# A retention and SwiGLU kernel on one core: the first head pair in chunks of 128 tokens, with its loads, weight roundings and first products reordered

## The chip, the cores and the metric

The kernel runs on one core of a Trainium2 chip. The core has a matmul engine (PE, whose weight loads are shown apart as PEld), a vector engine (DVE), an activation engine (ACT), a general engine (POOL) and a sequencer that mostly issues transfers (SP). Each engine works through its own list of instructions in order; semaphores order the engines among each other. PE writes only to PSUM, of which this kernel uses six tiles: four banks of 512 columns (bankA, bankB, bankC, bankE) and two of 1024 columns (inner and outer). Transfers are issued by SP, ACT and POOL and are carried by 16 DMA engines.

The metric is the time of one execution on the device, in microseconds (us). Every time below is in us unless it is marked otherwise.

## The reference, cut to what matters

The kernel computes a causal retention with a decay per head, puts the heads side by side, and feeds the result to a gated feed-forward block.

```python
# q, k, v: (8, 8, 576, 64) float32      batch, heads, tokens, head size
scores = scale * np.matmul(q, k.transpose(0, 1, 3, 2))
gamma = 1.0 - 2.0 ** (-5.0 - np.arange(H))
Dmat = np.where(rel >= 0, gamma[:, None, None] ** rel, 0.0)      # rel = row - column
attn_out = np.matmul(scores * Dmat, v)
x = attn_out.transpose(0, 2, 1, 3).reshape(B * S, H * D)         # (4608, 512)
g = x @ w_gate                                                   # (512, 1536)
out = (g / (1.0 + np.exp(-g)) * (x @ w_val)) @ w_out             # (1536, 512)
```

The three weight matrices arrive as 64-bit floats. The kernel makes 32-bit values out of them on the chip.

## The kernel before

**Tiles of tokens.** The 4608 tokens are worked in five tiles: a first one of 512 tokens, then four of 1024. The first tile uses plain matmuls and goes on while the weights still come in. The later ones use a scheme with fewer products and prepared sums of weights.

**Retention.** Heads are taken in pairs; the four pairs of a batch (HP = 4) fill the 128 partitions twice over. Pairs 0 to 3 belong to the first batch, and their first 512 tokens are the first tile. A pair is worked in chunks of 64 tokens (L = 64): scores inside a chunk, a state carried from chunk to chunk, and the share of all earlier chunks through that state. The functions are `transposes` (q and k are turned on PE with the identity, copied out of PSUM, and the keys are scaled by the decay), `scores`, `new_states`, `masked` (the decay mask on DVE and the chain of states), `own_values`, `earlier_values` and `to_x` (the copy into `xs[0]`, which holds the input of the feed-forward block, 128 features for each pair).

**Order at the start.** `tick(t, 0, HP)` for t from 0 to 5 is a pipeline over the four pairs: in tick t, pair t is turned, pair t-1 gets its scores and states, and pair t-2 its values. For pair 0 the copies, the scaling of keys and a copy of states are on DVE. For pairs 1 to 3 (`scaled`) the rows of q are scaled ahead of their transposes by POOL (`scale_run`, L735).

**Weights.** `load_w(m)` (L370) brings a quarter-megabyte or megabyte piece of the 64-bit weights into one of three raw places; the order of pieces is the list `order`, and I write w0, w1, and so on for its entries. `split(j)` takes half a piece apart with two activations (L389, L390) on ACT, and `rounding(j)` puts the halves together on DVE (L406, L407) and, unless it is told not to, goes on with `split(j+1)`. After the second half of a piece, `split` issues the load of the piece that takes its place. So w4 is issued by SP, behind the loads of pair 4, and w5, w6 and later ones by ACT.

**The first up stage.** `up0(f, chunks)` makes the products of output block f (12 of them, gate and value each) with the feature chunks named. A product of 128 features with 512 tokens is two PE rows in the trace. Blocks 0 and 2 and so on use bankA and bankB; blocks 1, 3 and so on bankC and bankE. With the last chunk it also issues the Silu (L856) and the product with the value half (L857), which free the two banks. Blocks 0 and 1 are started with chunks 0 and 1 amid the ticks, and finished with chunks 2 and 3 after them. Block 2 follows, then block 3, then the fifth pair's `new_states` and `scores`, then block 4. Blocks 2 and on need later pieces of the weights, and the fifth pair is loaded by `load(4)`, the sixth by `load(5)` (L282 and L287, both on SP).

**Order of issue.** The engines' lists are written out by hand: what stands earlier in the program stands earlier on its engine. Transfers issued by SP and ACT share eight completion semaphores. The trace shows that a transfer waits at issue until the previous one on the same semaphore has landed.

The lines below are at the center of both the change and the reading that follows.

Of the kernel before, what the change touches and what calls it, by code (L numbers as in the profile page):

```python
# [17 lines left out]
ALU = mybir.AluOpType  # L18
# [4 lines left out]
def tables(gamma, scale, L):  # L23

    g, at = np.array(gamma), np.arange(L)
    lane = np.arange(2 * L)[:, None]
    both = lambda t: np.repeat(t, L, axis=0).reshape(-1, 2 * L, t.shape[1]).transpose(1, 0, 2).reshape(2 * L, -1)
    twice = lambda t: np.concatenate([t, t])
    half = [np.repeat(g.reshape(-1, 2), L, axis=1).T ** (lane % 32 + 32 * r) for r in range(2)]
    pieces = scale * np.stack(half, axis=2).reshape(2 * L, -1)
    runs = scale * (g[None, :, None] ** ((4 * lane[:, :, None] + np.arange(4)) % L)).reshape(2 * L, -1)
    parts = [twice((g[:, None] ** -at).T), twice((g[:, None] ** (L - at)).T),
             both(g[:, None] ** L), both(g[:, None] ** (2 * L)), pieces, runs, both(scale * g[:, None] ** at),
             both((scale * g[:, None] ** at).reshape(-1, 2, L)[:, ::-1].reshape(-1, L))]  # L40
    return np.concatenate(parts, axis=1).astype(np.float32)
# [90 lines left out]
def kernel(  # L132
# [39 lines left out]
    L = D  # L172
# [74 lines left out]
    def scaled(i):  # L247

        return 0 < i < HP
# [4 lines left out]
    def load(i):  # L254
# [6 lines left out]
        if i < HP:  # L261
# [9 lines left out]
            for h, queue in zip(heads, queues):  # L271
                queue.dma_start(out=blocks(kn)[:, h % 2], in_=k[b, h, 0:CW].rearrange("(c p) d -> p c d", p=P))
            for h in heads:
                queues[i % 2].dma_start(out=blocks(t)[:, h % 2], in_=v[b, h, 0:CW].rearrange("(c p) d -> p c d", p=P))
        else:
# [33 lines left out]
    decays = nc.inline_tensor(table, name="decays").ap()  # L309
    NCOL = 6 * H + 4 * HP  # L310
    nc.sync.dma_start(out=tab[:, 0:NCOL], in_=decays[:, 0:NCOL])
    load(0)
    load(1)
    ident = const.tile([P, P], F32, name="ident")
    make_identity(nc, ident)
    nc.scalar.activation(out=io[:, 0:1], in_=ident[:, 0:1], func=AF.Silu)
    inv, key = tab[:, 0:H], tab[:, H : 2 * H]
    step = tab[:, 2 * H : 2 * H + 2 * HP]
    piece = tab[:, 2 * H + 2 * HP : 2 * H + 4 * HP]
    run = tab[:, 2 * H + 4 * HP : NCOL]  # L320
    qry, qry_odd = [tab[:, NCOL + HP * L * n : NCOL + HP * L * (n + 1)].rearrange("p (h i) -> p h i", h=HP) for n in range(2)]
# [9 lines left out]

    even_heads, odd_heads = slice(0, H, 2), slice(1, H, 2)
    for rows in half:
        decay(slice(0, H), slice(0, H), rows)

    load(2)
    nc.sync.dma_start(out=tab[:, NCOL:], in_=decays[:, NCOL:])
    load(3)

# [70 lines left out]

    for f in range(2):
        for m in range(2):
            load_w(m, (f,))
    load_w(2)
    load_w(3)

# [26 lines left out]

    def vector(i):

        return i == 0

    def transposes(i):
# [5 lines left out]

        copy = nc.scalar.copy if i else nc.vector.tensor_copy
        if i < HP:

            mine = (bankC, bankE) if i + 1 == HP else (bankB, bankA)
            parts = [(kT, kn, mine[0]), (qT, qk, mine[1])]
            if i == 0:  # L460
                parts.reverse()

            def turn(t, src, bank):
                for c in range(NFULL):
                    to = bank[:, c : 4 * P : NFULL] if t is qT and scaled(i) else bank[:, ts(c, P)]
                    nc.tensor.transpose(to, src[:, ts(c, P)], ident)

            def put(t, _, bank):
                if i or t is qT:
                    copy(t[:, 0:CW], bank)  # L470
                else:
                    copy(t[:, 0 : CW // 2], bank[:, 0 : CW // 2])
                    nc.scalar.copy(t[:, CW // 2 : CW], bank[:, CW // 2 :])

            if i + 1 == HP:
                for part in parts:
                    turn(*part)
                pieces = [lambda part=part: put(*part) for part in parts]
            else:
                for part in parts:  # L480
                    turn(*part)
                    put(*part)
        else:
# [12 lines left out]
        def keys():  # L496
# [5 lines left out]
            for hl, rows, at in parts:  # L502
                scale = key[rows, 2 * p + hl : 2 * p + hl + 1]
                if vector(i) or 1 < i < HP:
                    (nc.vector if vector(i) else nc.gpsimd).tensor_scalar(out=at, in0=at, scalar1=scale, scalar2=None, op0=ALU.mult)
                else:
                    nc.scalar.activation(out=at, in_=at, func=AF.Copy, scale=scale)

        if light(i):
            return [lambda: (keys(), pieces[0]())] + pieces[1:]  # L510
        return [keys] + pieces

# [63 lines left out]
    def masked(i):  # L576
# [6 lines left out]
        def copies():  # L583
            (nc.vector.tensor_copy if vector(i + 1) else nc.scalar.copy)(out=even, in_=z[:, 0])

# [144 lines left out]
    def scale_run(i):  # L730
        if scaled(i):
# [3 lines left out]
            nc.gpsimd.tensor_tensor(out=dst, in0=src, in1=table, op=ALU.mult)  # L735

    def tick(t, lo=HP, hi=NP, spread=False, then=None):
        go_on(len(pieces))
        if hi == HP:

            def new_pair():
                scores(t - 1, True)
                new_states(t - 1)
                pieces.extend(masked(t - 1))
                go_on(3)

            scale_run(t + 1)
            if lo < t < hi:
                new_pair()
            if lo <= t - 2 < hi:  # L750
                own_values(t - 2)
            for f in transposes(t) if lo <= t < hi and t + 1 < HP else ():
                f()
            if lo <= t - 2 < hi:
                earlier_values(t - 2)
                if t == HP:
                    up0(0, range(2))
                to_x(t - 2)[0]()
            if t + 1 == HP:
                split(0)  # L760
                after = transposes(t)
                rounding(0)
                for f in after:
                    f()
            if t == HP:
                rounding(2)
                rounding(3, False)
                new_pair()
                while held:
                    held.pop()()  # L770
                split(4)
                up0(1, range(2))
            return
        if lo <= t - 2 < hi:
# [66 lines left out]

    def up0(f, chunks):

        pair = banks[2 * (f % 2) : 2 * (f % 2) + 2]
        for gv, bank in enumerate(pair):
            for c in chunks:
# [577 lines left out]

    for t in range(HP + 2):
        tick(t, 0, HP)

        if t == 3:
            load(HP)
        for j in {3: (1,), 5: (4, 5)}.get(t, ()):  # L1430
            rounding(j)
    for c in range(2, HP):
# [133 lines left out]
```

## Time and profile before

| What | Value |
|---|---|
| Median of three runs | 1017.77 (1017.63 to 1018.7) |
| The profiled execution | 1019.25 |
| Its span, first to last instruction | 1017.5 |
| PE busy | 1001.9 (98% of the span) |
| DVE, POOL, ACT busy | 713.2, 564.4, 285.5 |
| DMA mean rate over the span | 191 GB/s |

The span is what the profile's views divide up, and 1.75 us lie around it in the profiled execution. A busy share of 98% doesn't mean that PE is always the limit: what an earlier start is worth is decided stage by stage, by which wait ends last. The page's second part cuts the span into 40 slices of 25.4 us, and PE is below nine tenths only in the first. The views used below are the table of stretches (busy time of each engine between two times), the list of waits, the chain of work that ended last, the list of instructions in order of time, and the DMA view of a stretch.

### The profile page before, as it was taken

The numbers are of one execution on the slowest core, as the hardware profiler recorded it, in microseconds if no ns is written. First come the engines' busy times: TensorE is split into PE (matmuls) and PEld (weight loads), VectorE is DVE, ScalarE is ACT, GpSimd is POOL, SyncE is SP. The second block draws the span as 40 slices with busy tenths as digits, with TensorE's granted clock in tenths as the row PEclk, the third lists the DMA queues.
The fourth block names the chain that finished last, engine by engine and source line by source line (L and its number), as shares of the span: only waits on it lengthen the run. The fifth ranks groups of instructions, "written<-read, shape, count | busy, mean of one in ns | idle before, by whom it ended". The sixth has DMA issues, their size and how long they took to land.

```text
span 1017.5 us, 21317 instructions
## 1 busy us (share of the span) xinstructions
PE 1001.9 (98%) x8336; PEld 825.5 (81%) x8336; DVE 713.2 (70%) x1203; ACT 285.5 (28%) x636; POOL 564.4 (55%) x591
## 2 busy tenths in 40 slices
PE   6999999999999999999999999999999999999998
PEld 5644455888888888888888888888888888888887
DVE  4478889678785765967768678866575767566644
ACT  4465622132423312133322101233320012232110
POOL 3400339979575318575565248756672586566515
PEclk9999999999999999999999999999999999999999
DMA  9999887777587887657677777434454554445653
GB/s 241 253 253 241 218 241 253 203 236 218 126 252 192 232 205 215 191 167 197 184 202 204 183 186 202 165 127 165 165 176 142 149 192 146 144 155 181 185 156 100
DMA packets 278892, 194.38 MB, mean 191 GB/s; under 512 B 212552, under 2 KB 246088, under 8 KB 278792
## 3 DMA queue, kind: packets, MB, share of 16 engines
q1 hardware_dynamic: 251464, 94.70, 36.5%
q10 hardware_dynamic: 26688, 97.92, 29.1%
q8 instruction: 66, 1.08, 0.5%
q0 software_dynamic: 640, 0.39, 0.2%
q14 instruction: 34, 0.28, 0.1%
HBM read 154.04 MB, written 38.93 MB: 190 GB/s over the span
## 4 chain that ended last, share of the span: by engine, by line
PE 83%; DMA 5%; DVE 4%; SPq 3%; ACT 2%; POOL 2%; issue 1%; ACTq 1%; DVEq 0%; POOLq 0%
PE bankB L1186 11%; PE bankC L1186 11%; PE bankA L1186 11%; PE bankE L1186 11%; PE bankB L1381 7%; PE bankC L1381 7%; PE bankE L1381 6%; PE bankA L1381 6%; PE inner L1186 2%; PE outer L1186 2%; DMA qk<-in_q_dram 1%; POOL rest L1042 1%; PE outer L532 1%; PE outer L559 1%; PE inner L573 1%
## 5 line engine op out<-in xcount | busy, mean ns | idle before, releaser
L1042 POOL TENSOR_TENSOR rest<-rest 128x512 f32<-128x512 f32 (+1 forms) x141 | 150.3, 1077 | 160.8 <-DVE rest L1042 113.2
L1201 POOL TENSOR_TENSOR arena<-rest,io 128x256 f32<-128x256 f32 x168 | 123.8, 748 | 90.9 <-ACT io L1200 86.3
L1200 ACT ACTIVATE io<-rest 128x256 f32<-128x256 f32 x192 | 79.1, 417 | 202.1 <-DVE rest L1042 134.1
L1186 PE MATMUL bankB<-rest,arena 128*128 128x256 f32 x448 | 114.7, 380 | 0.1
L1042 DVE TENSOR_TENSOR rest<-bankB,rest 128x512 f32<-128x512 f32 x116 | 78.6, 686 | 42.0 <-PE bankB L1186 29.5
L1186 PE MATMUL bankC<-rest,arena 128*128 128x256 f32 x416 | 106.4, 380 | 0.1
L1186 PE MATMUL bankA<-rest,arena 128*128 128x256 f32 x412 | 104.8, 379 | 0.0
L1042 DVE TENSOR_TENSOR rest<-bankC,rest 128x512 f32<-128x512 f32 x110 | 74.6, 685 | 39.3 <-PE bankC L1186 25.3
L1042 DVE TENSOR_TENSOR rest<-bankA,rest 128x512 f32<-128x512 f32 x110 | 74.6, 686 | 37.5 <-PE bankA L1186 18.9
L1042 DVE TENSOR_TENSOR rest<-bankE,rest 128x512 f32<-128x512 f32 x106 | 71.9, 685 | 36.8 <-PE bankE L1186 17.6
L1186 PE MATMUL bankE<-rest,arena 128*128 128x256 f32 x372 | 94.9, 380 | 0.6 <-DVE rest L1042 0.6
L1186 PEld LDWEIGHTS bankB<-rest,arena 128*128 128x128 f32 x448 | 84.6, 190 | 12.5 <-DVE rest L1042 0.7
L1186 PEld LDWEIGHTS bankC<-rest,arena 128*128 128x128 f32 x416 | 78.5, 190 | 11.9 <-DVE rest L1042 1.3
L1186 PEld LDWEIGHTS bankA<-rest,arena 128*128 128x128 f32 x412 | 78.1, 190 | 10.9 <-DVE rest L1042 0.2
L1186 PEld LDWEIGHTS bankE<-rest,arena 128*128 128x128 f32 x372 | 70.3, 190 | 10.7 <-DVE rest L1042 1.2
L1042 POOL TENSOR_TENSOR arena<-arena 128x256 f32<-128x256 f32 (+1 forms) x76 | 70.0, 943 | 9.0 <-PE bankC L1186 7.6
L886 POOL TENSOR_TENSOR rest<-rest 128x512 f32<-128x512 f32 x21 | 29.1, 1408 | 77.5 <-DVE rest L407 60.5
L1381 PE MATMUL bankB<-arena 128*128 128x256 f32 x264 | 61.0, 381 | 0.0
L1381 PE MATMUL bankE<-arena 128*128 128x256 f32 x264 | 60.8, 380 | 0.0
L1381 PEld LDWEIGHTS bankE<-arena 128*128 128x128 f32 x264 | 50.0, 190 | 6.9
L1381 PEld LDWEIGHTS bankB<-arena 128*128 128x128 f32 x264 | 49.8, 190 | 6.9
L1381 PE MATMUL bankA<-arena 128*128 128x256 f32 x240 | 55.3, 380 | 0.0
(267 smaller groups left out, 1879.0 us busy)
## 6 DMA issues: line engine op xcount, KB each, us to landing
arena<-up ACTq DMA_DIRECT2D x63, 896.0 KB, 4.7
arena<-dn ACTq DMA_DIRECT2D x65, 384.0 KB, 3.1
arena<-dn SPq DMA_DIRECT2D x39, 384.0 KB, 3.3
out_dram<-rest SPq DMA_DIRECT2D x31, 256.0 KB, 3.4
qk<-in_q_dram SPq DMA_DIRECT2D x108, 72.0 KB, 3.2
qk<-in_k_dram SPq DMA_DIRECT2D x108, 72.0 KB, 3.3
dn<-rest SPq DMA_DIRECT2D x26, 256.0 KB, 3.0
up<-arena SPq DMA_DIRECT2D x13, 512.0 KB, 5.8
```

What stands on the lines that cost most here:

```text
L532: m = nc.tensor.matmul(value(i, hl, c), s["v"][rows, at], ret[rows, c % 2 if whole(i) else hl, c // 2], start=start, stop=start, skip_grou ...
L559: nc.tensor.matmul(xr[half[hl]] if c + 1 == NC else value(i, hl, c), state[half[hl], c, :], s["qT"][half[hl], ts(c, L)], start=False, stop ...
L573: nc.tensor.matmul(sc[chunk(i, hl, 2 * c + r)[0], r if whole(i) else hl, c], kT[half[hl], at], qT[half[hl], at], start=True, stop=True, sk ...
L886: eng.tensor_tensor(out=dst, in0=srcs[0], in1=srcs[1], op=ALU.add if op[0] == "add" else ALU.subtract)
L1042: eng.tensor_tensor(out=out, in0=a, in1=b, op=ALU.add if sign > 0 else ALU.subtract)
L1186: m = nc.tensor.matmul(b[:, g * TB : (g + 1) * TB], w[:, g], x, start=(opens and g == 0), stop=True, skip_group_check=True)
L1200: nc.scalar.activation(out=s, in_=src[:, 0:TB], func=AF.Silu)
L1201: (nc.vector if busy and o != 2 and qd + 1 < NQ else nc.gpsimd).tensor_tensor(out=hid[:, qd, 2 * H + h, 2 * T + t], in0=src[:, TB : 2 * TB ...
L1381: nc.tensor.matmul(b[:, m * TB : (m + 1) * TB], lhs[:, qd, ts(m, P)], w[:, qd], start=(opens and qd == 0 and m == 0), stop=(qd == NQ - 1), ...
```

## The change

It touches the first 40 us of the program and nothing after it.

**Pair 0.** Three tables are added to the decay constants: `first_inv`, `first_key` (two columns each) and `first_qry` (128 columns). Pair 0 leaves the pipeline of ticks and gets functions of its own that use four chunks of 128 tokens where the others use eight of 64. `first_scores` turns q and k into bankE and bankC, multiplies q by `first_qry` while it is copied, scales the keys on DVE, and makes 8 score products of 128 by 128 in place of 16 of 64 by 64, masked in two DVE instructions with `first_near`, which POOL makes. `first_states` makes 8 state products into bankA, with one copy and three steps of the state chain. `first_own` makes 8 products, `first_out` 6, and one ACT copy puts the result into `xs[0]`.

**Loads.** The first table transfer moves behind pair 0's first q and k. The v loads of pairs 0 and 1 come after the q and k loads of both. Pair 3's loads come after the first halves of w0 and w1, and the second table transfer after w2.

**Order.** The ticks are replaced by a list written out. In it the transposes of pairs 1, 2 and 3 all go to bankC and bankE, and their two copies come ahead of the scaling of keys. The roundings of the first two halves come around pair 2's scores. The four products of block 0 with chunks 0 and 1 are spread: one ahead of pair 1's earlier values, two behind pair 3's transposes, one behind pair 2's earlier values.

```diff
@@ load(i), pairs 0 to 3
             for h, queue in zip(heads, queues):
                 queue.dma_start(out=blocks(kn)[:, h % 2], in_=k[b, h, 0:CW].rearrange("(c p) d -> p c d", p=P))
-            for h in heads:
-                queues[i % 2].dma_start(out=blocks(t)[:, h % 2], in_=v[b, h, 0:CW].rearrange("(c p) d -> p c d", p=P))
+                if i == 0 and queue is nc.sync:
+                    nc.sync.dma_start(out=tab[:, 0:NCOL], in_=decays[:, 0:NCOL])
+
+            def values():
+                for h in heads:
+                    queues[i % 2].dma_start(out=blocks(t)[:, h % 2], in_=v[b, h, 0:CW].rearrange("(c p) d -> p c d", p=P))
+
+            loaded[i] = (qk, kn, t)
+            return values
@@ set-up
-    NCOL = 6 * H + 4 * HP
-    nc.sync.dma_start(out=tab[:, 0:NCOL], in_=decays[:, 0:NCOL])
-    load(0)
-    load(1)
+    NCOL = 6 * H + 4 * HP + 4 + P
+    values = [load(0), load(1)]
     ident = const.tile([P, P], F32, name="ident")
     make_identity(nc, ident)
     nc.scalar.activation(out=io[:, 0:1], in_=ident[:, 0:1], func=AF.Silu)
+    for f in values:
+        f()
+    load(2)()
...
-    load(2)
-    nc.sync.dma_start(out=tab[:, NCOL:], in_=decays[:, NCOL:])
-    load(3)
...
-    for f in range(2):
-        for m in range(2):
-            load_w(m, (f,))
+    for m in range(2):
+        load_w(m, (0,))
+    load(3)()
+    for m in range(2):
+        load_w(m, (1,))
     load_w(2)
+    nc.sync.dma_start(out=tab[:, NCOL:], in_=decays[:, NCOL:])
     load_w(3)
@@ new functions for pair 0
+    def first_scores():
...
+        for src, bank in ((qk, bankE), (kn, bankC)):
+            for c in range(NFULL):
+                nc.tensor.transpose(bank[:, ts(c, P)], src[:, ts(c, P)], ident)
...
+        nc.vector.tensor_tensor(out=blocks(qT), in0=blocks(bankE), in1=table(first_qry), op=ALU.mult)
+        nc.vector.tensor_copy(kT[:, 0 : CW // 2], bankC[:, 0 : CW // 2])
+        nc.scalar.copy(kT[:, CW // 2 : CW], bankC[:, CW // 2 :])
...
+        for c, hl in first:
+            nc.tensor.matmul(inner[:, hl, ts(c, P)], kT[half[hl], ts(c, P)], qT[half[hl], ts(c, P)],
+                             start=True, stop=True, skip_group_check=True)
+        for hl in range(2):
+            nc.vector.tensor_tensor(out=first_ret[:, hl], in0=blocks(inner[:, hl]), in1=table(first_near[:, ts(hl, P)]), op=ALU.mult)
@@ the order of the start
-    for t in range(HP + 2):
-        tick(t, 0, HP)
-
-        if t == 3:
-            load(HP)
-        for j in {3: (1,), 5: (4, 5)}.get(t, ()):
-            rounding(j)
+    scale_run(1)
+    first_scores()
+    scale_run(2)
+    turn_pair(1)
+    first_states()
+    first_own()
+    new_pair(1)
+    turn_pair(2)
+    first_out()
+    split(0)
+    rounding(0, False)
+    scale_run(3)
+    new_pair(2)
+    own_values(1)
+    split(1)
+    up0(0, [0], [0])
+    earlier_values(1)
+    to_x(1)[0]()
+    put = transposes(3)
+    rounding(1, False)
+    for f in put:
+        f()
+    load(HP)
+    up0(0, [1], [0])
+    up0(0, [0], [1])
+    split(2)
+    own_values(2)
+    earlier_values(2)
+    up0(0, [1], [1])
+    to_x(2)[0]()
+    rounding(2)
+    rounding(3, False)
+    new_pair(3)
+    while held:
+        held.pop()()
+    split(4)
+    up0(1, range(2))
+    own_values(3)
+    earlier_values(3)
+    to_x(3)[0]()
+    for j in (4, 5):
+        rounding(j)
     for c in range(2, HP):
         for f in range(2):
             up0(f, [c])
```

## The prediction

> **What bounds the kernel now.** I read the table of stretches first, because a PE busy share of 98% hides where its few idle microseconds lie.
>
> ```profile
> core 0: us, PE busy (x) PEld busy (x) DVE busy (x) ACT busy (x) POOL busy (x), PEclk, DMA share, GB/s
> 0.00:4.40 4.40, 0.00 (x0) 0.01 (x1) 0.00 (x0) 0.00 (x0) 2.16 (x10) 1.00 0.62 138
> 4.40:23.00 18.60, 15.40 (x376) 12.93 (x376) 11.18 (x27) 8.79 (x19) 7.16 (x7) 1.00 1.16 259
> 23.00:41.00 18.00, 17.42 (x184) 8.93 (x185) 9.00 (x18) 11.16 (x24) 7.57 (x16) 1.00 1.00 269
> 41.00:58.00 17.00, 15.88 (x127) 11.93 (x126) 6.94 (x13) 6.90 (x14) 4.99 (x9) 1.00 0.90 187
> 58.00:127.00 69.00, 68.02 (x726) 34.47 (x724) 58.37 (x121) 42.31 (x79) 9.35 (x7) 1.00 0.94 249
> 127.00:1017.50 890.50, 885.17 (x6926) 757.18 (x6926) 627.74 (x1028) 216.37 (x505) 533.16 (x545) 1.00 0.62 184
> ```
>
> The DMA engines are as good as full from 4.4 to 58 (shares 1.16, 1.00, 0.90; transfers overlap, so a share can pass 1). PE loses 4.4 + 3.2 + 0.6 + 1.1 = 9.3 us there, and little later. So the change works on 9.3 us at most, and the transfers run full just where it wants to be faster. Next, PE's waits up to 60 us:
>
> ```profile
> PE bankA L466 <- POOL near L328: 4.4, 1, 4.4
> PE bankA L853 <- ACT io L856: 1.1, 1, 1.1
> PE outer L532 <- ACT rest L389: 1.1, 1, 1.1
> PE inner L573 <- ACT rest L470: 0.9, 2, 0.7
> ```
>
> The second row decides: it is at 57.41, where block 4 of the up stage begins, and an earlier start can be lost there. ACT's and PE's instructions around it:
>
> ```profile
> 52.80 0.67 ACT L389 ACTIVATE rest<-rest 128x512 f32<-128x512 f32 x1 [6.18 <-DMA rest<-in_moe_w_gate_dram]
> 55.63 0.69 ACT L389 ACTIVATE rest<-rest 128x512 f32<-128x512 f32 x1 [0.45 <-ACT rest L390]
> 56.77 0.59 ACT L856 ACTIVATE io<-bankA 128x512 f32<-128x512 f32 x1
> 57.41 3.70 PE L853 MATMUL bankA<-rest,arena 128*128 128x512 f32 x8 [1.12 <-ACT io L856]
> ```
>
> Block 4 needs bankA, which the Silu of block 2 reads. bankA was full at 44.8, but the Silu stands on ACT behind three splits, and the first of them waits for w4. The chain of waits has the same piece: w4's load, 43.95 to 52.69, then ACT.
>
> ```profile
> 41.31 2.54 SPq L287
> 43.86 0.05 issue
> 43.92 0.03 issue
> 43.95 8.74 DMA rest<-in_moe_w_gate_dram
> ```
>
> So block 4 starts at w4's landing plus 4.7 (57.41 - 52.69), if PE is there by then. PE was there at 56.3.
>
> **The change part by part.**
>
> *Pair 0.* Its 132 matmul rows become 68: 8 transposes stay, 32 + 32 + 32 + 28 become 16 + 16 + 16 + 12. Score products have half the number and twice the columns, so they cost the same (1.13 at the early pace). States fall from 1.08 to some 0.55, own values from 1.08 to 1.0, earlier values from 0.68 to 0.5: about 0.8 us of PE, in a stretch where PE idles 3.2. DVE trades one mask of 0.69, a pairing of 0.47, three chain steps and an evens step of 0.48 for two masks of 0.69, a copy of some 0.25 and three steps of 0.28; ACT loses a copy of 0.37. No DVE row shows a 512-wide copy with a table factor out of PSUM beyond the mask's 0.69, so I take 0.69; from the plain copy (also 0.69) to the slowest vector row of that size, 1.64, it lies between 0 and +1 us, hidden if block 4 stays the meeting point.
>
> *Loads.* SP and ACT issue the same transfers in another order. Near the start 128 KB land every 0.51 us. The first table grows from 64 to 196 columns: 68 KB, 0.27 us more for all that queues behind. It lands at about 5.6 and not 2.9, ahead of the copy that needs it (5.7). POOL waits for it too: new mask, two old ones (0.68 each), then pair 1's scaling at 7.7, which started at 8.58 before. Pair 3's q lands near 17.9 in place of 14.2, behind four weight quarters of 0.85 each; the halves of w0 and w1 needed first land near 15.3 and 17 in place of 19.7 and 21.2.
>
> *The walk to block 2*, with row durations, each engine in its new order. Pair 0's scores start at 6.9 (7.47 before): q landed 3.6, two sets of transposes of 1.09 each, copy by 6.4, half of k by 6.8. Pair 1 is turned by 10.2 (11.6); pair 0's states and own values follow to 11.8, then pair 1's scores (12.3 before). Pair 2's scores run at 16.3 (17.4). ACT then splits the first half (16.9 to 18.0; two rows start 0.57 apart), DVE rounds it by 19.1 (0.42 + 0.69). The first of the four products runs at 19.1, and only then pair 1's earlier values. Pair 3 is turned from 20.7 to 22.0, which is 0.8 later than before (20.1 to 21.2), as the product stands ahead of it. Two products follow by 23.7, pair 2's values by 25.1, the fourth product by 26.0. All four products lie in time in which PE waited or worked on the same four from 23.7 to 27.4. Pair 3's scores come at 26.0 (27.36), block 1's first products at 27.3 (29.05); their value half waits for ACT's fourth split and DVE until 28.5. Pair 3's values end at 32.1 (34.17), so block 2 starts at 39.0 in place of 41.14. Gain there: 2.1 us. Hidden in it: splits on ACT wait for weights with the copies of pairs 2 and 3 queued behind them; if the halves land 1 us later than I have them, 1 of the 2.1 goes.
>
> *What is late next.* PE would reach block 4 at 54.2. With w4 landing at 52.69 it would wait 3.2 there instead of 1.1, and the gain would be zero. So the sum is w4's landing. w4 stands on SP behind the same transfers as before (pairs 0 to 4, w0 to w3), w5 and w6 go on ACT's queue ahead of its landing as before, and the engines were full: order alone moves nothing. Two things do: the table's 68 KB, +0.27, and the program itself.
>
> ```profile
> q8 instruction: 66, 1.08, 0.5%
> q8 instruction: 1, 0.02, 0.9%
> ```
>
> The page's row is 66 transfers of 16 KB; PE's 16672 rows make 253 for each, so these are PE's instructions. The second row is the DMA view from 44 to 53: one block at 44.6, 0.9% of 16 engines for 9 us = 1.3 us of one engine, while w4 waits in line. w4's sixteen parts landed from 49.09 to 52.70, against 46.01 to 47.61 for the transfer just ahead: one engine lags. Pair 0 now has 264 - 136 = 128 fewer PE rows, half a block, so the block fetched at 44.6 is asked for some 128 rows later. Those rows end in the fifth pair's products at 55, behind w4. That takes 1.3 off the lagging engine if it is the one that fetched: between 0 and -1.3, and I take -1.3 because the lag grew by 2.0 just there. Sum: +0.27 - 1.3 = -1.0 us at w4 and at block 4. From 57.41 to 126 PE has no other wait, so I carry it to the end. Both ends of what is unknown: PE can gain no more than 1.1 + 2.1 = 3.2 at block 4; and a later w4 costs in full.
>
> [...] The rows give 259 and 269 GB/s with the engines full. [...]
>
> **The rivals.**
>
> *The whole start passes on.* If w4 lands 3 us or more sooner, PE's own time decides block 4: -3.2 us, 1014.6. For it: the share falls to 0.65 of full between 28 and 30, when SP is stuck behind a lagging engine, and w5 may be issued some 2 us sooner into that gap. Against it: the lag of that one engine never goes to zero from 15 to 53. [...]
>
> *A transfer's turn gets worse: slower.* SP and ACT share eight completion semaphores, and a transfer waits for the one that had its semaphore before.
>
> ```profile
> SPq L287 <- DMA rest<-in_moe_w_out_dram: 12.4, 2, 7.9
> ```
>
> Here pair 5's v load sat 7.9 us on SP until another load had landed; it landed at 70.2, and PE used it at 71.6. The new order deals the semaphores differently. If w4, or what stands ahead of it, waits so, w4's landing moves and block 4 with it, one for one; the new slack of PE doesn't help. It decides from a hold of 1.0 us, which takes back the forecast's gain, and ends above 0.2% from 3.0. The nearest rows are issues held 3.5 and 3.9 us on SP between 34 and 44. One more of 3.5: -1.0 + 3.5 = +2.5, 1020.3. Against it: most holds end in transfers that queue anyway.
>
> *The start isn't earlier at all*, ACT being held by splits that wait for weights. Up to 3.2 us of that costs nothing at block 4, so it ends with my forecast.
>
> **How the numbers follow.** The profiled execution took 1019.25 with a span of 1017.5; it is 1.48 above the median of the runs, 1017.77. Less 1.0: span 1016.5, profiled 1018.2, median 1016.8. That case, from no gain to -2.0 (1015.8 to 1017.8), gets 0.44, the whole start 0.31, the worse turn 0.25. The range has to reach into both: from 1013.9, the whole start with 0.7 us of the later wait at 127.28 (1.25, DVE's product) gone as well, to 1020.4. 0.2%, 2.0 us, is about what a measurement can tell from no change. Faster by more: 0.32; within: 0.44; slower by more: 0.24.
>
> **What would show it.** Right: block 2 starts near 39, PE's wait before block 4 grows to 2 us or more, still on the Silu, w4 lands near 51.7, and no 16 KB block is fetched between 40 and 52. Wrong: w4 landing before 50 or after 54, block 4 waiting for something other than that Silu, block 2 no earlier than 41, or a new PE wait between block 4 and 127 us.

## The result, and the profile after

The changed kernel takes 1024.38 us (median of 6 runs, 1021.61 to 1025.77) against 1017.70 for the kernel before on the same chip (6 runs). The ratio is 1.0069, with a 95% interval of 1.0056 to 1.0082. It is slower, by 5.7 to 8.3 us. The prediction was 1016.8, with a range up to 1020.4: wrong in size and in sign. The profiled execution took 1021.61, its span is 1019.9. It is the fastest of the six, and the one profiled before was slower than its median, so the two profiles differ by 2.4 us and show only a part of the loss. The rest has to be read from the profiles of the later runs.

The table of stretches of the changed kernel, with the columns of the one in the prediction:

```profile
4.40:23.00 18.60, 16.47 (x283) 12.68 (x282) 11.88 (x26) 9.79 (x20) 7.64 (x9) 1.00 1.15 255
23.00:41.00 18.00, 17.65 (x217) 8.85 (x216) 7.69 (x16) 10.41 (x22) 9.61 (x19) 1.00 1.08 251
41.00:58.00 17.00, 17.00 (x129) 12.35 (x128) 8.55 (x17) 8.04 (x15) 4.05 (x7) 1.00 1.12 262
58.00:127.00 69.00, 65.73 (x721) 33.80 (x720) 56.56 (x116) 40.72 (x77) 8.56 (x7) 1.00 0.97 237
127.00:1019.90 892.90, 885.94 (x6929) 757.64 (x6927) 628.33 (x1029) 216.97 (x506) 534.63 (x545) 1.00 0.63 183
```

Up to 58 us PE idles 2.8 us less than before, as it should. From 58 to 127 it idles 3.27 us where it idled 0.98 before. ACT's instructions, then PE's, around block 4 of the up stage, which was the meeting point:

```profile
50.91 0.67 ACT L398 ACTIVATE rest<-rest 128x512 f32<-128x512 f32 x1 [4.37 <-DMA rest<-in_moe_w_gate_dram]
53.80 0.67 ACT L398 ACTIVATE rest<-rest 128x512 f32<-128x512 f32 x1 [0.51 <-DMA qk<-in_k_dram]
54.95 0.59 ACT L869 ACTIVATE io<-bankA 128x512 f32<-128x512 f32 x1
```
```profile
55.61 1.55 PE L866 MATMUL bankA<-rest,arena 128*128 128x512 f32 x3
```

It is the same chain: w4 lands (50.80 now), three splits, the Silu, block 4 at 55.61 in place of 57.41. So at 57 us the changed kernel is 1.79 ahead. I lined up the two executions instruction by instruction from the end, where PE's programs are the same, and read the difference at each: -1.79 at block 4, the same up to 88.9, +1.93 at 90.8, +0.80 at 127.3 (a wait of 1.25 became 0.09), +2.14 at 420, +1.27 at 600, +2.38 from 625 to the end. The largest step is one wait. PE's waits from 58 to 130 us, and PE's instructions around that wait:

```profile
PE inner L559 <- issue: 3.3, 1, 3.3
```
```profile
88.53 0.22 PE L553 MATMUL outer<-qT,kT 64*64 64x64 f32 x1
88.58 0.28 PE L559 MATMUL inner<-qT,kT 64*64 64x64 f32 x3
92.13 0.68 PE L559 MATMUL inner<-qT,kT 64*64 64x64 f32 x27 [3.27 <-issue]
92.74 3.70 PE L866 MATMUL bankA<-rest,arena 128*128 128x512 f32 x8
```

PE stops amid the scores of pair 6, 27 matmuls from the end of them. "issue" means that the profile shows nothing that it waits for. The DMA view of 88 to 92.2 us has one row of interest:

```profile
q8 instruction: 1, 0.02, 1.6%
```

That is one 16 KB block of PE's program. Its transfer starts at 89.71, after PE has stopped; 2.42 us later PE goes on. This suggests theory A: **PE ran out of program.** Its rows (matmuls and weight loads) follow each other here at some 120 a us, so a block of 256 instructions is run through in some 2 us, and the next had not come. The rival B: the new order of loads and steps holds PE by something that the profile doesn't show.

### The profile page after: what moved, and what is told of

The parts are those of the page before. It is cut to its first block, busy times and chain, and to the rows that moved or that the text cites. A ratio compares the mean times of both kernels' runs of the same rounds, so it can differ in the third digit from the quotient of the medians.

```text
span 1019.9 us, 21185 instructions
## 1 busy us (share of the span) xinstructions
PE 1003.1 (98%) x8272; PEld 825.7 (81%) x8272; DVE 713.0 (70%) x1200; ACT 285.9 (28%) x636; POOL 565.4 (55%) x592
## 3 DMA queue, kind: packets, MB, share of 16 engines
q8 instruction: 65, 1.06, 0.4%
## 4 chain that ended last, share of the span: by engine, by line
PE 91%; DVE 2%; DMA 2%; POOL 1%; SPq 1%; issue 1%; ACT 1%; ACTq 0%; DVEq 0%; POOLq 0%
PE bankB L1199 11%; PE bankC L1199 11%; PE bankA L1199 11%; PE bankE L1199 11%; PE bankB L1394 7%; PE bankC L1394 7%; PE bankE L1394 6%; PE bankA L1394 6%; PE outer L1199 2%; PE inner L1199 2%; PE outer L518 2%; PE bankA L866 2%; PE bankB L866 2%; PE inner L559 1%; PE outer L545 1%; PE bankE L866 1%
```

## The experiments

**Moving the block ends.** The edit puts small products that nothing reads ahead of everything on PE; 32 of them are 128 PE instructions, half a block. They run while PE waits for its first load.

```diff
+    for n in range(32):                      # 16, 48, 64 in the other runs
+        a, b, c = n % 2, n // 2 % 2, n // 4 % 4
+        nc.tensor.matmul(outer[half[b], a, ts(c, L)], ident[half[a], 0:L], ident[half[a], L : 2 * L],
+                         start=True, stop=True, skip_group_check=True)
```

Kernel before with 128 rows:

> The kernel before with 32 dummy products of 64 by 64 (identity by identity into outer, overwritten later) at the head of PE's program, where PE waits 4.4 us for the first load anyway: 128 PE instructions more and nothing else. Theory A (the loss is where the 16 KB program blocks end): half a block of shift puts a block end into the dense products near 88 us with another one less than a block behind it, as the change does; PE sits 2 to 4 us idle there with no releaser, and the time is 3 to 7 us above before. Rival B (the loss comes from the new order of loads and work at the start): the dummies lie in idle time, within 1 us of before.

Changed kernel with 128, with 64 and, run again, with none:

> The changed kernel with the same 32 dummy products, so that every later PE instruction stands where it stood before in its program block. Theory A: the 3.27 us wait near 89 is gone, a block is fetched near 44 again and w4 lands near 52.5 as before; 0 to 1.5 us below before, so 1016 to 1018. Rival B: as the changed kernel, 1022 to 1026.

> The changed kernel with 16 dummy products, 64 PE instructions, a quarter of a block. Theory A: only one block end falls into the dense products near 88, and the block fetched at 44.6 before the change is still asked for behind w4: no wait near 89, w4 near 51, block 4 near 55.7; 1015 to 1017, below before. Rival B: as the changed kernel, 1022 to 1026.

> The changed kernel once more, for a second trace. Its six runs lay between 1021.61 and 1025.77 and the profile shown was the fastest. Theory A: the wait near 89 is there again, and where a run takes 1024 or more it is longer than 3.3 us, or the granted clock falls behind it. Rival B: no wait without a releaser that is longer than 1 us, the time is lost elsewhere.

And with 256 rows, a whole block, for both, and 192 for the changed kernel:

> The kernel before with 256 PE rows that compute nothing that is read (64 products of 64 columns) ahead of its first transposes: block ends fall on the same instructions as before, one block later. With 128 such rows it was 2.1 us slower. Theory A (where blocks end decides): back to within 1 us of before, 1015.5 to 1017.5. Rival (the rows cost by themselves, or any shift of the fetches does): 2 to 4 us slower.

> The changed kernel with 256 such rows ahead of the first transposes: block ends fall on the same instructions as in the changed kernel, and PE does the same later. With 128 rows it took 1019.0, with 64 rows 1021.7, with none 1023.2. Theory A: 1022 to 1025, as with none. Rival (what helps is that PE comes later and waits less, by the length of the padding): at or below the 1019.0 of 128 rows.

> The changed kernel with 192 such rows ahead of the first transposes. The wait put down to nothing came at the same row, 1985, in three of four profiles with the changed kernel's blocks; with 192 rows more, blocks end 96 rows into the dense stretch near 88 us and right behind its end, so no whole block lies in it. Theory A: no such wait near 89 us, 1018.5 to 1021.5. Rival (only 128 rows happen to help): 1022 to 1025.

Measured, each against the kernel before on its own chip:

| rows added | kernel before | changed kernel |
|---|---|---|
| 0 | 1 | 1.0069, 1.0082 [1.0059, 1.0105] |
| 64 | | 1.0060 [1.0045, 1.0075] |
| 128 | 1.0023 [1.0010, 1.0036] | 1.0026 [1.0009, 1.0043], 1.0045 [1.0029, 1.0060] |
| 192 | | 1.0086 [1.0070, 1.0102] |
| 256 | 1.0011 [1.0002, 1.0021] | 1.0079 [1.0064, 1.0094] |

(1.001 is 1.0 us. The second value at 128 is from the last group of runs, and its expectation is printed there.) The same 128 rows make the kernel before slower and the changed one faster, and 256 rows bring the changed kernel back to 1.008. So it is not that PE starts later or does more: the position within a block of 256 matters. Between 128 and 256 rows it is worth 3.4 to 5.3 us, between 64 and 256 rows only 1.9.

Five expectations fell.

- The kernel before with 128 rows lost 2.1 us and not 3 to 7. Its profile has no wait near 88 us; the only one put down to nothing, 1.90 us, is at 620.
- The changed kernel with 128 rows took 1019.02 and not 1016 to 1018.
- With 64 rows it took 1021.68 and not 1015 to 1017, although its profile has no wait near 89, as expected.
- Run again without rows (1023.15), its profile has no wait near 89 either.
- 192 rows were meant to be harmless. There the wait stood at the very end of the stretch (2.99 us at 96.21): a whole block lay in it all the same, and the next one was late for the products behind it.

The first and the fourth show that block ends alone do not make the wait. The kernel before with 128 rows has its block ends in this stretch within two instructions of where the changed kernel has them. There and in the changed kernel run again, the transfer of the block started at 83.33 and 84.90, some 3 us before PE entered the block ahead of it (86.70 and 87.79). In the profiles with the wait it started 3.5 to 5.1 us after that point. Why it starts early in some executions was not shown.

The wait itself, in the changed kernel with 256 rows:

```profile
94.79 1.11 PE L559 MATMUL inner<-qT,kT 64*64 64x64 f32 x27 [4.96 <-issue]
```

It is at the same product as in the changed kernel, 27 before the end of the scores. Counting PE's instructions in the order of the trace (weight loads, matmuls and its semaphore instructions), it comes behind number 1985 without the rows and 2241 with them. In the 20 profiles of this study PE has 27 waits of more than 0.3 us that are put down to "issue". All 27 are behind an instruction whose number leaves 193 when it is divided by 256. That settles what they are: ends of blocks of 256 instructions, which come in transfers of 16 KB. In none of the 20 profiles does a block's transfer start more than 299 instructions ahead of the block's first one, which is a block and 43 instructions.

**The wait by itself.** 192 of the same products (768 instructions, three blocks) at three places of the kernel before, fenced so that they wait for PE alone:

```diff
+        if f == 5:
+            plan.append(dense)
         plan.append(lambda f=f: up0(f, range(HP)))
...
+    dense()
     for n in range(1, NTILE):
+        if n + 1 == NTILE:
+            dense()
```

> The kernel before with 192 small products (768 PE rows, three 16 KB blocks) that nothing reads and that wait for nothing but PE itself, at three places: near 81 us (DMA engines full), after the first tile's down stage near 160 us (DMA share about 0.66) and at the start of the last tile (share about 0.5). The changed kernel's dense stretch ran some 120 rows a us, so three blocks take 6 us if nothing holds them. Theory A (PE runs out of program where rows follow each other faster than blocks arrive): waits of PE put down to nothing in each place, 2 to 5 us a block near 81 us and 0.5 to 1.5 us a block where the DMA engines have room. Rival (the 3.3 us near 89 us in the changed kernel were another hidden wait): no such wait in any of the three, and the span longer by some 18 us only.

One execution was taken, of 1057.41 us, against 1016.6 for the kernel before on that chip. The products came to lie at 63, 192 and 845 us. PE's instructions at the first two places, then the stretches around them:

```profile
63.26 2.44 PE L1457 MATMUL outer<-ident 64*64 64x64 f32 x151 [0.15 <-PE bankB L860]
71.20 3.69 PE L1457 MATMUL outer<-ident 64*64 64x64 f32 x128 [5.50 <-issue]
78.77 3.05 PE L1457 MATMUL outer<-ident 64*64 64x64 f32 x105 [3.87 <-issue]
...
191.61 2.32 PE L1457 MATMUL outer<-ident 64*64 64x64 f32 x143 [0.15 <-PE bankE L871]
195.06 2.09 PE L1457 MATMUL outer<-ident 64*64 64x64 f32 x128 [1.13 <-issue]
198.51 1.90 PE L1457 MATMUL outer<-ident 64*64 64x64 f32 x113 [1.36 <-issue]
```
```profile
63.00:81.00 18.00, 8.48 (x365) 8.07 (x368) 8.16 (x17) 6.60 (x11) 0.00 (x0) 0.75 1.07 250
190.00:201.00 11.00, 8.21 (x390) 6.75 (x389) 2.82 (x3) 1.56 (x3) 10.69 (x13) 1.00 0.33 124
```

Between two waits lie 128 matmuls with their 128 weight loads: one block. With the DMA engines full (share 1.07) a block is waited for 5.50 and 3.87 us; with engines that have nothing else between 193 and 199 us, 1.13 and 1.36. There the block's transfer starts 1.13 us after PE entered the block ahead of it, and PE can use it 2.32 us later: 3.45 us, against the 2.09 in which it runs through a block. With full engines the transfer started 4.5 and 5.1 us after that point. So theory A stands for this wait, and at these two places a block is waited for longer where the DMA engines are full. The third place misses the expectation: 4.62 us at 852. The mean share is about 0.5 in that stage, but the engines were full from 847.5 to 851 (share 0.97), while the block was on order. What the wait goes with there is the load on the engines in those few us, not its mean.

**Blocks moved only behind w4.** The 128 rows are put ahead of the steps before block 4 instead of the start, between two fences.

```diff
     assert not todo
+    (the 32 products)
     for f in plan:
         f()
```

> The changed kernel with 128 PE rows that compute nothing that is read (32 small products) after block 3 of the up stage, just ahead of the dense steps before block 4, near 54.5 us. Up to there the blocks are those of the changed kernel (no block ahead of w4's landing), after it those of the kernel before. Theory A: no wait put down to nothing near 89 or 625 us; the rows cost about 1 us; 1018 to 1020. Rival (the changed kernel loses by its order of work and loads after 55 us, whatever the blocks): 1022 to 1025.

1021.3, 1.0052 [1.0035, 1.0068]. No wait near 89 or 625, as expected; the time lies between the two expectations. As with 64 rows, moving the blocks removes the wait, but not all of the loss.

**Cutting the dense stretch**, with the blocks where they are:

```diff
+            if t == HP + 2:
+                up0(6, range(HP), [0])
             scores(t - 1, t - 2 < lo)
```

> The changed kernel with the eight gate products of up step 6 (3.6 us of 512-wide products, 16 PE rows) moved up into the dense stretch near 88 us, between pair 5's earlier values and pair 6's scores. Rows, their number and the block ends are those of the changed kernel; only no block is run through in 2 us there any more. Theory A (the wait near 89 is a block that is run through faster than the next one comes): no wait put down to nothing between 85 and 97 us, and the 3 to 5 us of it, with the half-speed clock behind it, are gone: 1018.5 to 1021. Rival (the wait has another cause in the order of loads and goes elsewhere, as in the second profile of the changed kernel, where it stood near 107): 1022 to 1025.

1024.0, 1.0071 [1.0047, 1.0096]. The edit did not do what this says: the products came into the stretch near 71 us, since the one near 88 belongs to the tick behind it. The latter was left whole, and the wait was there again, 4.35 us behind number 1985. So that the wait goes when the stretch is cut was not tried. What it adds is a count: of the five profiles with the changed kernel's block ends, four have the wait there. The fifth (the changed kernel run again) got its block at 84.90, ahead of the stretch, and had its loss elsewhere, as shown below. The kernel before with 128 rows, with the same block ends, has no wait there either.

**The order of loads**, first alone in each kernel:

```diff
-    for f in range(2):
-        for m in range(2):
-            load_w(m, (f,))
+    for m in range(2):
+        load_w(m, (0,))
+    load(3)()
+    for m in range(2):
+        load_w(m, (1,))
     load_w(2)
+    nc.sync.dma_start(out=tab[:, NCOL:], in_=decays[:, NCOL:])
     load_w(3)
```

> The kernel before with the new order of loads alone (first table behind pair 0's keys, values after the first four loads, pair 3 between the weight halves, second table behind w2). PE's program, and so where its 16 KB blocks end, is that of before. Theory 'blocks and PE's new order' (the loss comes from pair 0's fewer rows and the moved steps): within 1.5 us of before. Theory 'loads' (the loss left with 128 rows put back, some 2.6 us, is the loads' order): 2 to 4 us slower than before, with a wait of PE near 104 or 128 us that before does not have.

> The changed kernel with the old order of loads (the first table keeps its new width). PE's program is that of the changed kernel. Theory 'loads': 2 to 4 us faster than the changed kernel, 1019.5 to 1021.5. Theory 'blocks and PE's new order': 1022 to 1025 as the changed kernel.

The kernel before with the new loads: 1028.03, 1.0110 [1.0093, 1.0127]. The changed kernel with the old loads: 1025.92, 1.0093 [1.0076, 1.0110]. Neither theory had 12 us for the first; the second came out just above both of its ranges. PE's wait, and what DVE stood at:

```profile
PE outer L540 <- DVE rest L653: 9.0, 1, 9.0
```
```profile
30.46 1.29 DVE L653 TENSOR_TENSOR rest<-outer,tab 128x256 f32<-128x256 f32 x3 [12.72 <-DMA tab<-decays]
```

Pair 0's old output step multiplies by the second decay table, which the new order puts behind w2. Pair 0 by chunks has no such step, so the new order of loads needs the new pair 0. Around this wait the granted clock was 0.50 for 17.07 us, which may be why the loss is larger than the wait. The second run has the 4.06 us block wait at number 1985 again, and so says nothing about the loads. Both orders therefore had to be compared with the blocks moved.

**The parts, with blocks as in the kernel before.** All have pair 0 by chunks and the 128 rows at the front. The old order of loads is the diff above the other way round; the old order of steps is this, with the pairs' other steps as they were:

```diff
-    rounding(0, False)
-    split(1)
-    up0(0, [0], [0])
-    rounding(1, False)
-    up0(0, [1], [0])
-    up0(0, [0], [1])
-    split(2)
-    up0(0, [1], [1])
+    rounding(0)                 # behind transposes(3), and going on with split(1)
+    rounding(1)
+    up0(0, range(2))            # behind earlier_values(2)
```

> Pair 0 by chunks of 128 tokens alone: the changed kernel's pair 0 with the old order of loads (the first table keeps its new width), the old order of roundings and the four products in one piece, and 128 rows ahead of the first transposes, which put the blocks where the kernel before has them. Theory C (what is left beside the blocks comes from the new orders, not from pair 0): 1015.5 to 1018. Rival (pair 0 itself costs): 1019 or more.

> As the run before, but with the new order of steps (roundings sooner, the products spread), still with the old order of loads. Theory C: 1018.5 to 1022, as the halves are split before their loads are due. Rival (only the blocks made the old loads with the new steps slow, 1025.9): 1017.5 or less.

> New order of loads, old order of steps, pair 0 by chunks, 128 rows ahead. With the old pair 0 this order of loads gave 1028.0, with a wait of 9 us near 32 us, as DVE stood at a rounding whose half came later. Theory C: 1020 to 1029, the wait near 30 us again. Rival (pair 0's chunks were what the new loads needed): 1019 or less.

> The changed kernel with 128 rows ahead of the first transposes, again, beside the other three: new loads, new steps. 1019.0 in its first runs, of which the profiled one had 1.7 us from a half-speed clock. Theory C: 1018.5 to 1020.5, without a wait put down to nothing near 89 or 625 us; waits near 105 and 128 us of 0.5 us or more. Rival (the first runs were lucky, as the other block positions without that wait gave 1021 to 1022): 1020.5 to 1022.

And one, run earlier, with the new orders but for the four products of the first up step, which are in one piece behind pair 2's earlier values:

> The changed kernel with 128 rows ahead of the first transposes (1019.0 so far) and, in addition, the four products of the first up step in one piece again, behind pair 2's earlier values. Theory 'the moved products are part of the 3 us that the 128 rows leave over the kernel before': 1017.5 or less. Rival (what is left lies in the loads' landings and the waits of Silu and DVE near 105 and 128 us): 1018.3 to 1020.5.

| loads | steps | us | ratio |
|---|---|---|---|
| old | old | 1020.96 | 1.0039 [1.0025, 1.0052] |
| old | new | 1019.14 | 1.0032 [1.0020, 1.0044] |
| new | old | 1019.18 | 1.0019 [1.0009, 1.0029] |
| new | new | 1020.60 | 1.0045 [1.0029, 1.0060] |
| new | new, products in one piece | 1021.83 | 1.0056 [1.0041, 1.0071] |

The reason that the third expectation gives for the 9 us was wrong (it was the table, not a rounding), and the wait did not come. Theory C falls: pair 0 by chunks alone, with the old orders, is no nearer to the kernel before than with the new ones. The repeat with 128 rows, 1020.60, came out on its rival's side, and the four products in one piece above both of their ranges. The changed kernel with the old loads went from 1.0093 to 1.0032 by nothing but the 128 rows. What is left in these five is 1.9 to 5.7 us (6.1 with the 64 rows), of which the rows themselves may be the 1.1 to 1.3 that 256 of them cost the kernel before.

**What the rest goes with.** Three 512-wide products that nothing reads were put ahead of block 4 in the changed kernel with 128 rows:

```diff
+    for n in range(3):
+        nc.tensor.matmul(outer[:, 0, :], ident, xs[0][:, n, :], start=True, stop=True, skip_group_check=True)
     for f in plan:
```

> The changed kernel with 128 rows ahead of the first transposes (1019.0 in its runs, profiled in one of the slower ones), and three 512-wide products that nothing reads just ahead of block 4's dense steps, 1.3 us of PE. Theory 'what is left is PE coming early to the waits near 105 and 128 us, which the transfers' landings set, and the half-speed clock that a long wait brings': the 1.3 us are taken from those waits, no half-speed window near 130, and the time is no longer, 1016.5 to 1019. Rival (PE's own time decides there): 1.3 us longer, 1020 to 1021.5.

1021.29, 1.0039 [1.0026, 1.0052], and the waits near 105 and 128 us were no shorter: 1.64 and 2.04, against 0.80 and 1.91 in one profile with the 128 rows alone and 1.58 and 2.18 in the other. So PE's being early is not their cause; but against 1.0026 and 1.0045 the added 1.3 us don't show in the time either. In this execution pair 7's keys landed at 100.58. They are what block 10 near 105 us hangs on: ACT scales them, splits four half pieces of weights and only then makes the Silu of block 8 that frees bankA. In the kernel before, keys at 97.01, Silu at 103.68, block 10 at 104.64, with 0.4 us to spare. ACT's scaling of these keys in the best and in the worst of the four runs above (new loads with old steps, new with new), then PE's waits of the worst and the first of them in its place:

```profile
92.82 0.96 ACT L493 ACTIVATE kn<-kn,tab 128x256 f32<-128x256 f32 x2
```
```profile
102.34 0.96 ACT L493 ACTIVATE kn<-kn,tab 128x256 f32<-128x256 f32 x2 [5.02 <-DMA kn<-in_k_dram]
```
```profile
PE bankA L866 <- ACT io L869: 6.1, 2, 4.5
PE bankE L877 <- DVE arena L870: 2.2, 1, 2.2
```
```profile
59.10 3.46 PE L866 MATMUL bankA<-rest,arena 128*128 128x512 f32 x4 [4.53 <-ACT io L869]
```

The first execution took 1017.89, with no such wait; the second 1025.37. Of the 6.1 us on bankA in the second, only 1.58 are at block 10. The other 4.53 are at block 4, as w4 landed at 54.41 there, so that this execution was 3.4 us behind the kernel before at 90 us already. Over twelve profiled executions, both kernels among them, the landing of pair 7's keys (92.3 to 102.3) and the time (1017.35 to 1025.37) go together with a correlation of 0.93, some 0.7 us for each us. (They are all those with no block wait of 1.3 us or more, but for the kernel before with the new loads, which stood 9 us for its table.) When what each lost up to 90 us is taken off both, the correlation is still 0.90. It differs as much between executions of one kernel: the changed kernel with 128 rows had 97.34 and 102.32. The kernels before have 97.0 and 93.2, ten others 92.3 to 102.3. That the landing is what costs, and not a third thing that sets both, was not shown; nor which part of the change delays it. One candidate is on record: SP's issue of these keys was held 5.0 us in the worst execution, and 4.4 in the changed kernel run again, until a weight load with the same semaphore had landed. But it was held 3.7 us in the best of the four too.

**The clock.** Behind some of the waits lies a second loss. The changed kernel run again, which had no wait near 89, waits for block 8's Silu instead; the three stretches before, in and after what follows:

```profile
107.58 2.08 PE L866 MATMUL bankA<-rest,arena 128*128 128x512 f32 x2 [2.97 <-ACT io L869]
```
```profile
100.00:107.33 7.33, 4.60 (x11) 1.71 (x9) 5.33 (x12) 5.99 (x11) 0.00 (x0) 1.00 0.90 215
107.33:110.74 3.41, 3.16 (x4) 1.51 (x5) 3.02 (x6) 2.85 (x6) 0.00 (x0) 0.50 1.17 309
110.74:115.00 4.26, 4.26 (x11) 1.89 (x10) 2.96 (x5) 2.94 (x6) 1.37 (x1) 1.00 1.06 380
```

The granted clock is 0.50 for 3.41 us. By an estimate this costs half of that, 1.7, where PE has work all the time. The profile of the kernel before has no such window once its clock is up; with the waits of 4.06 and 4.96 us come two of them, 6.83 us.

## Why the prediction was wrong

- **Block 4 as the meeting point, and w4's landing plus the Silu's 4.7:** right. 50.80 and 55.61 are 4.8 apart.
- **w4 lands 1.0 sooner, as no program block is fetched ahead of it:** the fetch moved as foreseen (blocks at 35.23 and 58.51, none between), and w4 landed 1.9 sooner. That was luck. Run again, with the blocks in the same place, w4 landed at 52.42, and the kernel before with the three dense places, whose block came at 45.85, had it at 50.83. Leaving out the kernel before with the new loads, the seven profiles with no block between 40 us and w4 have it at 50.80 to 54.25, the twelve with one at 50.83 to 54.41. Neither the 1.3 us of the block nor the table's 0.27 is shown by any run; the landing moves by more than both from one execution to the next.
- **Block 2 at 39.0:** it came at 40.43. PE had a wait of 1.06 at 18.83, which is one of the 27 block ends, and pair 0 was mis-sized. Its score products before, then now:

```profile
7.47 1.13 PE L573 MATMUL inner<-rest,kT 64*64 64x64 f32 x32 [0.52 <-DVE kT L472]
```
```profile
6.83 2.59 PE L744 MATMUL inner<-rest,kT 64*128 64x128 f32 x16 [0.55 <-DVE kT L738]
```

The working's "half the number and twice the columns, so they cost the same" left out how many rows start together. In the traces four of the 64 by 64 rows start every 0.11 us, but two of the new ones every 0.21; the wait for ACT's half of k makes 0.34 of the 2.59. Pair 0's states, own values and earlier values start in twos as well, every 0.10 to 0.11 us, so half the rows save nothing. The four groups of products took 5.6 us, where the working had 3.2 and the kernel before 4.0. As the prediction had it, this cost nothing at block 4.
- **"From 57.41 to 126 PE has no other wait, so I carry it to the end":** this is the step that failed. It was true of the kernel before, whose blocks ended elsewhere. The working counted the 128 rows that the change takes away, and used them to move a fetch past w4, but saw a block only as a transfer in w4's way, and not as what PE itself waits for in the next dense stretch. PE stood 3.0 to 5.0 us for such a block in the profiles with it, and the runs with 128 rows in place of 256 put it at 3.4 to 5.3 us of the time. The other part of the step failed too: in seven of the ten profiles of changed kernels in which no block was late between 58 and 130 us, PE waited 0.4 to 3.0 us at block 10 near 105. That hangs on a landing, as block 4 does, with 0.4 us to spare in the kernel before. What remains without the block wait, 1.9 to 6.1 us, goes with the landing of pair 7's keys; its cause stays open.
- **The rival with the worse turn of a load** had the sign, but not by what the runs show: the block wait has no load's turn in it. Whether such a turn is in what remains, at pair 7's keys and not at w4, stays open. "A new PE wait between block 4 and 127 us" was named as what would make the prediction wrong, and it did.
- **The range** had no case in which PE's program comes late, so no bound for it, and ended 4 us short.

## What to carry to other kernels

When an edit adds or removes matmuls, it moves every later block end of PE's program. Find the stretches in which some 120 PE instructions run in a us, and count to the 256-instruction boundaries in them; a wait put down to nothing in any profile of the program gives the offset. A block that lies wholly within such a stretch cost 1.1 to 1.4 us here with idle DMA engines, and 3 to 5.5 with full ones when its transfer came late, which it did in four of the six profiles with the changed kernel's block ends. Before judging such an edit, measure it again with half a block of idle rows at the front. And a gain at one wait that hangs on transfers is worth no more than the slack at the next: take the list of all waits and near misses, not the one that is longest. And when products are made fewer and larger, look in the trace at how many of each shape start together before taking their cost as equal.

## What the runs showed of the hardware

- Where PE stood waiting, a 16 KB block of its program took 2.2 to 3.1 us from the start of its transfer until PE ran it. In the eight waits of 2.9 us or more the transfer started 3.5 to 5.1 us after PE had entered the block ahead; with DMA engines that were idle or nearly so, 0.8 and 1.1.
- A wait of 1.91 us was followed by 3.41 us at a granted clock of 0.50 (the changed kernel with 128 rows, near 129), while after one of 3.27 us in the changed kernel the clock stayed at 1.00. So of these two waits the shorter one cost a window and the longer one did not; what decides it was not shown.
- The same load of one program landed 5 us apart in two executions (pair 7's keys in the changed kernel with 128 rows, 97.34 and 102.32), which took 1020.43 and 1025.37.
